# Cross terms of a long convolution added by accumulating transfers, with one pool for product and spectrum buffers and a new order of work

## The chip, the cores and the metric

The kernel runs on one core of a Trainium2 chip. The metric is device time in microseconds (us), the median of several runs. Runs fall into a fast and a slow state (of four, three at a mean granted clock of 0.972 to 0.976, one at 0.84); only fast runs are compared here (the ratios and their intervals; a median given below takes in all runs), and where a trace fell in the slow state, it is said. The granted clock is the share of TensorE's full clock that the profile shows as granted; in the stretches below it lies between 0.50 and 1.00. In this kernel TensorE does the matrix products (PE in the profile, 1780 matmuls in before) into the accumulators called PSUM, the Vector engine (DVE) mostly elementwise work on two inputs (272 of its 406 instructions), the Scalar engine (ACT) activations and evacuations of PSUM (copies out of it), SyncE (SP) and GpSimd (Pool) issue most of the transfers (229 and 16 in before).

## The reference, cut to what matters

A sequence of 2048 positions by 640 channels goes through layer norm, a gated long convolution by Fourier transform, and a SwiGLU feed-forward network (FFN), with residuals:

```python
kv  = shift_conv(k) * v
y   = irfft(rfft(pad(kv)) * rfft(pad(ssm_k)))[:2048] + kv * ssm_D
h   = x + layernorm(x) * y
out = h + (silu(ln(h) @ w_gate) * (ln(h) @ w_up)) @ w_down
```

## The kernel before

The sequence is cut into four blocks (0 to 3), each with its share of convolution and an FFN of 14 feature tiles. Block j's output spectrum is a sum of products of input spectra X and filter spectra (A and B, cut from K) of the blocks up to it. Each transform has two stages on TensorE with a shuffle between them: an on-chip transfer of 160 KB, because the second stage wants other rows together. Names below: `shK21G1` is the shuffle of K, block 2, half 1 of the columns, piece G1 of four; `s2K21G1` the second-stage matmuls that read it; `rs10G2` a shuffle on the way back in block 1; `i1100` the matmuls that read that. These names are the program's; the trace calls all such transfers `sb<-sb`, and they are told apart by their place in their queue, which the program fixes. The shuffled pieces live in rings of three buffers:

```python
P.pool("UK", slots(3, 2 * CW), True)      # shuffled pieces of K, given out in order
P.pool("UX", slots(3, 2 * CW), True)      # shuffled pieces of X
P.pool("E",  slots(5, HW))                # swapped spectra
P.pool("PP", slots(3, HW))                # products
```

Products are multiplied and summed on DVE. `extra` is a cross term that block 2 (the third) computed ahead for block 3 (the fourth), by the eight adds named q4 and q6:

```python
def prods(nm, terms, h, prio, extra=None):
    acc = None
    for n, (a, b_) in enumerate(terms):
        p = (P.tile(f"P{nm}{n}", "PP"), 0)
        ew(p, a, b_, ALU.mult, h, prio, f"m{nm}{n}")
        ...                                # the first is acc, later ones are added on DVE
    if extra is not None:
        ew(acc, acc, extra, ALU.add, h, prio, f"x{nm}")
    return acc
# block 2, after its own sums:
ew(x1, x1, r, ALU.add, h, pr + 5, f"q4{nm}")
ew(a1, a1, q, ALU.add, h, pr + 5, f"q6{nm}")
```

The program isn't written in the order in which it runs. A table in the file gives each of 1219 operations an engine and a planned start time, presumably found by a search outside the chip (the code carries an estimated cost for every operation); the code replays that table: it sorts each engine's instructions by it, hands out pool buffers in that sequence, and adds semaphores. Up to the first FFN, a group of matmuls with a planned wait ahead of it gets filler matmuls. So each engine does its work strictly in the order of the table.

## Time and profile before

| | before |
|---|---|
| median of 4 runs beside the changed kernel | 312.83 us (310.87 to 313.86) |
| span of the profiled run | 308.7 us |
| PE busy, of it filler | 283.5 us, 19.4 us |
| DVE, ACT, Pool busy | 234.8, 187.1, 27.0 us |

The prediction below shows the lines behind this table. For what follows it helps to cut the span at the same points of the program in both kernels: at the first FFN matmul, at the last matmul of `dn0310`, at the first matmul of the third FFN, and at the last matmul of all. `dn0310` ends the down product of one of the first FFN's four row groups; two of the others follow some 10 us later. The stretch up to it is called the first FFN stage below.

### The profile page before, as it was taken

To read this page: it belongs to the slowest core of one execution; us is meant where nothing else is said; L and a number is where in the kernel's file an instruction comes from. 1 tells how busy PE (TensorE), PEld (TensorE's weight loads), DVE (VectorE), ACT (ScalarE), POOL (GpSimd) and SP (SyncE) were. 2 spreads that over 40 slices of the span, in tenths; PEclk is the share of its full clock that TensorE was granted. 3 is DMA by queue.
4 is the path that set the end of the run, shared out by engine and by line. 5 is a ranking of instruction groups with operands and counts; after the bars stand their busy time and mean duration, and the time that the engine had idled before them with its cause. 6 is when DMAs were issued, how large, how long until landed. Compare 5 with 4: busy or idle time off the path is not lost.

```text
span 308.7 us, 4989 instructions
## 1 busy us (share of the span) xinstructions
PE 283.5 (92%) x1780; PEld 167.9 (54%) x1780; DVE 234.8 (76%) x406; ACT 187.1 (61%) x280; POOL 27.0 (9%) x34
## 2 busy tenths in 40 slices
...
GB/s 219 342 193 297 237 220 236 222 142 298 253 274 290 293 268 266 167 252 216 197 236 42 127 227 53 127 151 206 199 111 82 46 46 81 2 0 0 2 85 44
DMA packets 53116, 52.09 MB, mean 169 GB/s; under 512 B 21202, under 2 KB 46163, under 8 KB 53092
## 3 DMA queue, kind: packets, MB, share of 16 engines
...
q10 hardware_dynamic: 1010, 0.79, 0.8%
...
## 4 chain that ended last, share of the span: by engine, by line
PE 62%; DMA 14%; DVE 7%; ACT 7%; SPq 4%; issue 3%; POOL 0%; ACTq 0%; DVEq 0%
PE ps L492 58%; DMA sb<-sb 11%; DVE sb L501 6%; SPq L483 4%; ACT sb L475 3%; PE ps L515 3%; DMA sb<-in_A_ssm_k_dram 2%; DMA sb<-in_A_q_dram 1%; ACT sb L478 1%; ACT sb L778 1%; PE ps L624 1%; ACT sb L790 1%; DVE stt L755 1%; DVE sb L777 0%; POOL stt L768 0%
## 5 line engine op out<-in xcount | busy, mean ns | idle before, releaser
L492 PE MATMUL ps<-sb 128*128 128x320 bf16 (+3 forms) x1128 | 208.9, 336 | 1.1 <-DVE sb L501 1.1
L501 DVE TENSOR_TENSOR sb<-sb 128x1280 bf16<-128x1280 bf16 (+2 forms) x238 | 174.1, 767 | 15.8 <-ACT sb L475 4.7
L492 PEld LDWEIGHTS ps<-sb 128*128 128x128 bf16 (+2 forms) x1128 | 108.6, 98 | 82.3 <-issue 4.7
L475 ACT ACTIVATE sb<-ps 128x640 bf16<-128x640 f32 x131 | 88.7, 712 | 39.1 <-PE ps L492 37.3
L492 PE MATMUL ps<-sb,tab 128*128 128x320 bf16 x450 | 78.2, 303 | 10.3 <-DMA sb<-sb 7.5
L492 PEld LDWEIGHTS ps<-sb,tab 128*128 128x128 f16 x450 | 42.3, 98 | 38.1 <-DMA sb<-sb 7.7
L501 DVE TENSOR_TENSOR sb<-ps,sb 128x640 bf16<-128x640 f32 (+3 forms) x34 | 29.1, 857 | 41.9 <-PE ps L492 40.4
L1034 ACT ACTIVATE sb<-ps 128x1024 bf16<-128x1024 f32 (+2 forms) x32 | 29.3, 916 | 23.7 <-PE ps L492 23.5
L778 ACT ACTIVATE sb<-sb,stt 128x320 bf16<-128x320 bf16 (+1 forms) x34 | 24.0, 728 | 7.1 <-DVE stt L770 4.8
L478 ACT ACTIVATE sb<-ps 128x640 bf16<-128x640 f32 x31 | 21.0, 704 | 10.5 <-PE ps L492 10.4
L515 PE MATMUL ps<-sb 128*128 128x192 bf16 x158 | 19.4, 270 | 7.3 <-ACT sb L475 4.2
L755 DVE BATCH_NORM_STATS2 stt<-sb 128x6 f32<-128x320 bf16 x48 | 22.3, 484 | 0.2
L1050 ACT ACTIVATE sb<-ps 128x1024 bf16<-128x1024 f32 x18 | 18.4, 1025 | 5.6 <-PE ps L492 4.9
L515 PEld LDWEIGHTS ps<-sb 128*128 128x128 bf16 x158 | 14.4, 107 | 12.9 <-ACT sb L475 7.6
L768 POOL TENSOR_TENSOR stt<-stt 128x2 f32<-128x2 f32 (+1 forms) x10 | 11.4, 1138 | 52.6 <-DVE stt L766 42.1
L476 DVE CAST sb<-ps 128x640 bf16<-128x640 f32 (+1 forms) x8 | 6.2, 779 | 7.9 <-PE ps L492 7.9
L804 POOL TENSOR_TENSOR stt<-stt 128x4 f32<-128x4 f32 x2 | 2.6, 1297 | 77.4 <-DVE stt L802 77.4
L790 ACT ACTIVATE sb<-sb 128x640 bf16<-128x640 bf16 x8 | 6.0, 744 | 2.3 <-DMA sb<-in_A_q_dram 2.3
L797 ACT ACTIVATE sb<-sb,stt 128x640 bf16<-128x640 bf16 x8 | 6.6, 832 | 0.0
L777 DVE TENSOR_SCALAR sb<-sb,stt 128x320 bf16<-128x320 bf16 (+1 forms) x14 | 5.5, 395 | 0.9 <-DMA sb<-sb 0.5
L483 POOL DMA_DIRECT2D sb<-in_B_w_down_dram x3 | 2.1, 698 | 32.9 <-DVE sb L501 29.0
L483 POOL DMA_DIRECT2D sb<-in_A_k_dram x2 | 2.1, 1028 | 26.8 <-DVE stt L759 26.8
...
## 6 DMA issues: line engine op xcount, KB each, us to landing
sb<-sb SPq DMA_DIRECT2D x144, 160.0 KB, 2.3
out_dram<-sb SPq DMA_DIRECT2D x16, 160.0 KB, 1.9
...
sb<-in_A_v_dram POOLq DMA_DIRECT2D x4, 320.0 KB, 4.4
...
```

Of the source, the lines that this page charges most:

```text
L475: fns = {"act": lambda a: a.activation(out=dst(), in_=src(), func=ACTF.Copy), "dve": lambda v: v.tensor_copy(out=dst(), in_=src())}
L478: fns = {"act": lambda a: a.activation(out=dst(), in_=src(), func=ACTF.Copy, scale=scale), "dve": lambda v: v.tensor_scalar(out=dst(), in0 ...
L483: fns = [(lambda g, d=d, s=s: g.dma_start(d(), s())) for d, s in subs]
L492: return lambda t: t.matmul(o(), l(), r(), start=st, stop=sp)
L501: return lambda v: v.tensor_tensor(out=o(), in0=a(), in1=b_(), op=op)
L515: P.fill = lambda t, pt: t.matmul(B32(pt, 1, 192), V(GUT, 13 * 512 + 256, 128), V(GUT, 13 * 512, 192), start=True, stop=True)
L755: vec(dve1(CW, False), lambda v: v.bn_stats(st6(l, j, b, c), V(xt, b * D + c * CW, CW)), [(xt, (b, c))], [(ST, ("s", j % 2, b, c))], prio, ...
L768: P.op({"pool": 0.95}, lambda g: g.tensor_tensor(out=y, in0=va, in1=stt[:, 288:288 + hi - lo], op=ALU.pow), c1 + [(ST, "half")], c3, prio, ...
L778: "act": lambda a: a.activation(out=dst(), in_=src(), func=ACTF.Identity, scale=rs(l, j, b), bias=tmv(l, j, 3)[:, b:b + 1])},
L790: P.op({"act": act_c(D) + 0.22}, lambda a, b=b, jt=jt: a.activation(out=V(jt, 0, D), in_=V(xt, b * D, D), func=ACTF.Copy, accum_out=tmv(l, ...
L1034: P.op({"act": act_c(n)}, lambda a: a.activation(out=dst(), in_=src(), func=ACTF.Silu), rd, wr, -1000, name=f"si{j}{i}")
L1050: P.op({"act": act_c(1024)}, lambda a: a.activation(out=V(ut, 0, 1024), in_=B32x2(u, 512), func=ACTF.Copy), [(u, 0), (u, 1)], [(ut, 0)], - ...
```

## The change

Its intent is to relieve DVE: the sixteen adds of cross terms become transfers that add in flight into their destination, issued from Pool. Product and spectrum buffers come from one pool of eight, because a product now lives longer (until the transfer has read it: from issue to landing such a transfer took 3.5 to 7.25 us in the trace of after, where an add on DVE took 0.79 in before). And there is a new order for all of it. The diff, cut:

```diff
+    DACC = "xq"
-        P.pool("E", slots(5, HW))
-        P.pool("PP", slots(3, HW))
+        P.pool("E", slots(8, HW))
+        def acc_dma(dst, a, h, prio, nm):
+            P.op({"pool": 1.0}, [lambda g: g.dma_start(V(dst[0], dst[1], HW), V(a[0], a[1], HW), accum_op=ALU.add)],
+                 cells(a, h) + cells(dst, h), cells(dst, h), prio, dma=(328, 2560), name=nm)
-                p = (P.tile(f"P{nm}{n}", "PP"), 0)
+                p = (P.tile(f"P{nm}{n}", "E"), 0)
-                ew(acc, acc, extra, ALU.add, h, prio, f"x{nm}")
+                if "x" in DACC: acc_dma(acc, extra, h, prio, f"acx{nm}")
+                else: ew(acc, acc, extra, ALU.add, h, prio, f"x{nm}")
-                ew(x1, x1, r, ALU.add, h, pr + 5, f"q4{nm}")
+                (acc_dma(x1, r, ..., f"acq4{nm}") if "q" in DACC else ew(x1, x1, r, ...))
...                                        # q6 likewise; one setup instruction is put first on its engine
 _ORDER = (                                # the whole table is new
```

More of the change, by code (lines that the diff above doesn't have):

```diff
@@ L128, in replay @@
                     self.pools[tl.pool].free.append((max(p.finish for p in tl.touch), tl.base, tl.touch))
+        q = self.order[self.warm.eng]
+        q.remove(self.warm)
+        q.insert(0, self.warm)
+        for i, o in enumerate(q):
+            o.pos = i
         end, cold = 0.6, 6.9
@@ L716, in prods @@
                 else:
-                    ew(acc, acc, p, ALU.add, h, prio, f"a{nm}{n}")
+                    if nm[1] in DACC:
+                        acc_dma(acc, p, h, prio, f"ac{nm}{n}")
+                    else:
+                        ew(acc, acc, p, ALU.add, h, prio, f"a{nm}{n}")
             if extra is not None:
-                ew(acc, acc, extra, ALU.add, h, prio, f"x{nm}")
+                if "x" in DACC:
+                    acc_dma(acc, extra, h, prio, f"acx{nm}")
+                else:
+                    ew(acc, acc, extra, ALU.add, h, prio, f"x{nm}")
             return acc
@@ L915, in conv_half @@
                 x1, a1 = sX(1), sA(1)
-                q = (P.tile(f"q{nm}", "PP"), 0)
+                q = (P.tile(f"q{nm}", "E"), 0)
                 ew(q, x1, Bw, ALU.mult, h, pr + 5, f"q1{nm}")
                 ew(x1, x1, A, ALU.mult, h, pr + 5, f"q2{nm}")
-                r = (P.tile(f"r{nm}", "PP"), 0)
+                r = (P.tile(f"r{nm}", "E"), 0)
                 ew(r, X, a1, ALU.mult, h, pr + 5, f"q3{nm}")
-                ew(x1, x1, r, ALU.add, h, pr + 5, f"q4{nm}")
+                (acc_dma(x1, r, h, pr + 5, f"acq4{nm}") if "q" in DACC else ew(x1, x1, r, ALU.add, h, pr + 5, f"q4{nm}"))
                 ew(a1, Xw, a1, ALU.mult, h, pr + 5, f"q5{nm}")
-                ew(a1, a1, q, ALU.add, h, pr + 5, f"q6{nm}")
+                (acc_dma(a1, q, h, pr + 5, f"acq6{nm}") if "q" in DACC else ew(a1, a1, q, ALU.add, h, pr + 5, f"q6{nm}"))
         def conv_bp(j, c, bp, HTt, pr):
@@ L1127 @@
 _ORDER = (
-    "c-pO030PBC7A7x`kdOtkhwLj^$i4sx*~tb3LLh`B2#6?%vRJFFindy}X>Bc4i+qk&#tpYBE|t1f9c|UNRIS#PDq2NtYf-0)wiPG1b!_X@nXmV}@0|0_yZ4-X"
-    "{`=ntfDi~2h=Dv101AQ+ofrrRg+M_F2!g;<1Ny{!v?eOi0Y3J@fe!=rsX+8CS|?^;*(3A&EKepr$4cnH3*^y$qG1pUjcz^qfDa5b=Fxyafafz&JzxOvH|k+p"
-    "=(8~Rb*~`!4F7SPPj&WG6nNCi<CgwBIq>|+A%Bp30KJE^9(sQbQs9FzKnCD}dKOB+A2#)$jCcUbQ|x%=gkRfwUhMv~B=CQfjN%A9Mils~5Pity=Rowo@a|dU"
-    "co+vj$m1p;{~Lb5?+O5qejC4u1AoXr;0gbtr5>UM{HcBxPD^4UF)JaFm;qS?xdN$z@PP_|2|Ws70+sPCG2cU+z*t~DZ~?%BI`DWb1@<AN4^|IpM7g1#K@Y@)"
@@ L1132 @@
-    "AR@@Su|2UII0|f!<Hvp!TM8D#uE1YMyoTsS-bT_<+tI^;4FC*U58Vr$4xRxqus$FH{SsuvB4Wd_T~HL*2X%vIW0%D?!M=kB;-<#M!>7Xc!kvimu%BUK#A!rx"
-    "{I&SiNG^(xtVeD|DiKo<Y4KI@Juo*s2tNtm5Z{Dyqb{S==t*cMx*ok9U6Y_mIE&em5W=p-9mMWQ>`QFJ+`vx5y+b;OuY!4Fcfhc5)o~}|vf+#2TyQFQBX(C@"
-    "ZfpSNMRX#zB9_EAz(=F^qF=!5z#tR*6S5NLB{sw%;RW%%@%xd3P!VJgQjZj)M<wpZl5v%|d)NZpIoxdAQT%OuKH(cefH;x39P1=ZBJL;FkhYSpl9mxS5V0f*"
-    "X%gu?$wj_RT1mb|9zu?gH<GuJ&yh<g4U{&DFlkKEJxmvA5<W~_OJBeik&tW{OV8RT=w{Cn9TFWBy&-8%dV%^fC4*X?1X8zAI+J!%ebkw>9NIoAg1(k+rb`*k"
@@ L1136 @@
-    "%#T=KbB;4;tWxemRu{KlP$BH)mk7=a>y!PW@k|QiJ8l;DF0+<*m-jJG#qSiJN-h_y7nO)5Y$zunTEl*ubCz>lBolukX_QvUa#df;7RvLLe)S%;RdGP^qjIcj"
-    "s``j{M~XpqL_SNk1cr&P1PQ1%v@BsV;uNYEGlv2}Yccl|P?$+b7`2)X#qJ?rV|UQMrVr)n5!d1GAb9cT;<d;X$bRI@apSOOuu4oH=5S&S_7>WL5#Z+F|AAxR"
-    "C!u@Lqfp0C0rYBg5vm2H#H_{CV>%Ot<6H0(2_1xK37ZmhiPIBz6TeJE5;JgYQVsbS?jZR(B_nA@5}PuT0#Ntk;|Ws2M8dp88TJ#xZNdS9gSeP_g=(hlOxjKf"
-    "Qafk>y^B7UzMD>EjN@+QuHgK_q3~Yk>G%qvfe-Q*@vrcmf-M4Ja!Yb4W(9_vP?sP~+?JStos2z<XOl*fwvgtNgQPanb|Q>qrS40rr*Ecdar<xpQB7Qgi^1E7"
@@ L1140 @@
-    "qlhojjHH`1CH)5)gRZ2N)21;tGgeY5v=F18v5O969$^k;-DY{&vw5TVSNS2{0iIBBn47};fZNNBVHL5KvhJ|P@;>5}@|UqU@#_S?@XrcblVQRm!V$@zCeIbV"
-    "B1Ve)M0Rnv*e}tf?2(j8Orj=9w`5t$MCmo@dKpnlmyVUzN#{z5vhU?@$XXPO<svypK3P6q{+_&2L02{@<|v8EpR}{J2K5)J3A*iSK`KZ4fo6ZICT)rKXqrkd"
-    "*Zfm$PyZ@yo#v+gvSD|IK7(LhX}V~9*DSV1Qa{vvZWwI%HnlN>Yr2@eM9;IVvE&)n*)(>e=@ny#In#XHL^Ch5Fzl~p@*JS+kmrJ9gj4K-dC*xkR-p}-33rq_"
-    "I$g8e*`8j{xojM^pIk;BLD|S+ayDppqz_7+lBP(P=(F{Bqt(=7xNahuTg|!nW_%oB0U>$?DPR(s`U<s~UC0^5+0E%>Q#gwmy^K1(fqRZyB)r6=vh2*!%u?q2"
@@ L1144 @@
-    "%$Y0=dkuf7V3;6IykF2KIL7A-E(kQqPT|<-O}N2J5cMScl8c2`g>Q*);#T2&F<dfEGCk$1l!-E5%7T=ODW9h-lYT3qDoRrLQoZO!(H8L~ak;cz%9Q2FVr2G|"
-    "ZL*UxhD<5{n|!3=o?^42P`O4KqpDD?RmG&vSCKTjv|TEh<_pa#?O^R(-Om=4^;=_{xzXBbZLq^LH(GC5-Nsc$hV8fwY45i0rPb5nj55Y1hL`z1%fvY^*e&8n"
-    "u1HVI+GHeoSh7q~A&)4WYPw>Iyj{*$1QZVG80j$idBs6hf+|jZUwujmSM5|fR0}kE-3oQT_Pkc7ou<2}hO1xFbm>;70%;Ygp|tk2*z|Sj7=4?$R^Jgl!TISP"
-    "!+rgGh7U5_M!$ZG9%EQ-kQ(cZ%QH@7+%jxU?J)8(YBTyXVl5F%lkt?X%v5ZC-+aSrw9T-otxK)ftPWeDv)i)K^_Fdndz{T_Uv9r{w`PvXJeS##>31y5?6ONU"
@@ L1148 @@
-    "8y)Qqg7c!I)-lF`aypzf&d;6QQF+sq;L33tow=@K&b!VEm*2h0HN%Z?AMy?HHRPSin~`7PyPZES2bD9^+njqRr#g@1qj@p8Tm0Gnw{zbt$O<0ySh6zm+ww`-"
-    "R)1Q-)WY6EZBc8{Yk@;SOR+lpldPWLgkVL^{9<H?Txcpd5a=tcEkp-q7P&(ohjSx`BB;88;=`d(SQPo9c6;QrlC08COW9?aC4oU*gGx)w%9b;IiosH@w8T0&"
-    "ZG=~wzc=qfJ~7YjUsQO~uPzV;t^_bedy9T#zssR<=W;E)cHZCBH?<}WKXqN|;<PF0RXS&y#9+<Pm@b*OSza(rG2bvR)E(DxObbj4%~DIM^^RqyGsX6{WtW9)"
-    "t+wuW+;+enX^wq1n{%f--?PGVBI{>Yde-bLcJ^1<f}Hl8#o1T0wK*79o$IDk<?8TU_7FUo9-^l*yC$2K1A4>WCEjg0cf7f|K;9i+W`26!)Vy8!DaF%+C4r=("
@@ L1152 @@
-    "#^UwG?$9^ICyGuK%?X?haDuJDW5Ic0vNl_nm)@OTr*AXOx7WDVn|f>$?ai*ATulzOv)vYNAD#1#N9XIyD{^<aN4Z<wYqHK{DLk)w1ld32Ov#se|K;W8-p>hm"
-    "FXl9PC*-cqZOpr$+nE=W*Xq0FGv^ok=H>hRs|tQBI1%VBP!<x4@ctIR+`rJzEqJlO?c3qI=08yIgFm^jvCv$!uP`gHIB+X~4i*QO1T%wkgWbV<!HVM3#e&e-"
-    "(5etDd^WT;bRmQdRfOc>Vc{L&OX1RRFpQ4872X)05Sbm7oe@I`Cz2GQl#GtFM4|^+(qGb1q8+5IY^~fmOkBkoy1MFm#k7j%DxiAQkk_iK%V(F7E7lCYT;5WF"
-    "9y)%gYxu_DcZX_fEQ61hpRTU2-Zi*n_@E&NhWLkF8tSS1au~O4OX*K#OUqKrCYCjpvuZZgY#nK+ZK}-}v2TQTWamh3ZCc%~y3O^e4YL}OYuDAf>krm58~zP&"
@@ L1156 @@
-    "9!w_"
+    "c-pO02Ut`07Ef+MAdpFRLM9<QAtZq?l8`|LGm~tPEusuJj#jI6(W-T|%2Qjdt94ShrNgT4QLUqj)LE^I;?}yWw!ov-`s`=ldp+mgbIv{YjQ{!F^IZT6215W)"
+    "4}(Eq2o&0_dQE5#^+@0k1bJrt7T6uy&7eMp_Pl`hUN1Pn-95UgPd!)VC7Hl82l%;6FzC5c^gTd&++YX<0`0xJ?;ZyA5x6_`FR5<XqX6g&qK6=Vj=}F!LZL6S"
+    "f!|VJz~m3!?gN1P<^w<9=2gYPf2lb5KZ|!`)_1TT^q|nc1t~}`QV?)A0lfn9-wXnMej}j0-@dy5<mCat?*Rb#f5z^GmcVZ<fmfUfcqyU)`0qy)^8X;(x2KSv"
+    "YQW3<eItRMq53NPfIhqTU-4q0e@FB!{2v><46SGT*JJfU0lZTF8BSb85HuGQ1XX~NfM{S8un7DkxC-0?J_2R{LC}2AKfxWq17H?FhO_|`NC;Q~Gy{)-dteZ<"
@@ new lines @@
+    "D?$x!0|~%;fls4zqBq9aBZ*N>F+W9|ifTuGgWQ8OMGr%tM1jzI&<BB1$W{mvS_a()&55AF1d#C%6%-sX5ZVmwiXg)%P<uo<>>b#;NJ<nrYH!qy$eB@#qnPlw"
+    "VOt_8@FCF;qFZ7f$5;@fV^R@sB5I@WL{E+07X1)5CNc&tkI}^}K`4<;$S$N3wG+uj4Mtr>A4kJ69?XK+{jp};8q5{!VYEG#j$44o5{AN-M!+IRM(&T)Ma_wd"
+    "fKP^g4=suCz^WqMQ4<hrkv9>8k&B|9AT209dI<VGOeJ~)I)G_}<D;RlRv08^C;}9{9`Qa}jD}#}!**hov8C8G*n8Luv9&l6ZXWImj*0KW&&IXkuH$U@o%l(F"
+    "Fku!xjgU_$B#b7UCdh~;;`c-`DL`})w-cuk*AcO#4$@>&8hH|V3hFD&Oj0Eo#+b>RL3$TIgockp#XsWb#rp(yae`zp`6y*OsXt{Ri9lIJUQDr5f1-@0U8Ihp"
@@ new lines @@
+    "9;XeWRnh`+yXoe*mN*(?E}g|#$S`rxyia(lga*EX4-*_0w6e#svN#<~EvKDhjUU0K$Bz@-=ilSLE@~Ek&JZz|#b+{CGjB0ha$ALFkx?c~yr-C!7%N|$q*iQG"
+    "G|M?jWW@r7N|`8uOE1Z2^3jTqVGWTtpkE;j_$9IP;F~FTV`1b{;+I4h?H%G;!ihKx`wLb*bsVRJJ()d+vkV@BKZF}%PR95Vml0!;d*DCCdU5x#AH^<2b1-W#"
+    "_c3R1OK{T(bi5L^5Y>qyqVFS1P^(cVQ8Y{``X~m6{f-bxY$UW1_}JRmCd_usF5*7I7TT9oTO5ztNdAR3mGOX4!lctL&=)hEw4Jmf!gRv6SSqd(_Y{YSvl6@F"
+    "hLOh5BN?;eMzAW`8`yFVjO}ILX4l4_=VWr5xEHu<69_`RU_P&m$KcQ4w+OVtbwZ}-9BMXdEcy;Q54#i#i@ivghd)E!N<mONsYdE*>P=DxIgXx0OJxV?d6Y2}"
@@ new lines @@
+    "Dk+ELCmtkfh;xZUsUk)_Z9d(|8p0YyUquHo8kp}gPcvItBiN7F|6)yyZ{|GZd=o#0caXP~|AgyGsNiF`dhR*yjD#IbGHY7=_V{B75H6iZ;11<2;iLKY`ISP1"
+    "$R~mcy~25-<AM{S7V*#GTuG~>P%4$GB{tDvNxbwm=_cuB*%j$p>2m1>=_x57tCY=_ol3kdi;<5^JS_vs-%4yr#LGv?1@efbsq%};4-|t`$5gGVK=RkgHudt9"
+    "&g3!4ywvIxW;#OIsC<~ZFzunTCjEGNqlT(A>y~P7Yxn35WcpGstE19ar=!!}%iw4g88<Ve`ufZc&076P(*k{qj%8S5fEx-7Q;a*Tmu$<kSLc9ohgyENjItff"
+    "*5y7jY%@yC2h0yGb4<>xgXRv)7uk=nBPd76$y7I|j)O~nBXwZfeDyCW%hK7I;0%R!tj4Wx)F&H0BPEh|l8KZ-l+zSA&B3T<e2{P@VFTw*{P6@n?-C~|elYJW"
@@ new lines @@
+    "e?8A5yuzZg%UNq#0?vHS682U0I4(nQjW=6(ieDzUBA^Nj`Fr_Ggx?Ae2|tKCBI*#1q}oKYM3+PkaW(s>c&Oxpq)kee)u?85qsW&HlFdoP$uRPZvb@A{!6Ly{"
+    "NvC9=jG4Gzc3w6iNh5ulR4HF4pPyt;x}J1dabJE|NmDhb+$kTXG^w+aHz&8LmC9*KXv)BpV9LRiCc_8=J@bpq8-^0&>8!e}9Am5TWF}9KG&xL<O;WRhzKZdL"
+    ";bux%Bz6lsCLt`?FCvS}#cRb6#I+Kr*dyL1;U?dcTvAO^Y*O%LURhn@Ub#E*recV4l}e)8km^*8S2d;VN|CC=YOMOQ8l~Q#RHY`XucoxA(^J1m9iNt#+>sVa"
+    "CuHo%h|m=4FKCLiEd9+4i-w!_siru?rzz6R)V!ae*G$oF(F%1<x(gavdb@6=_Lydd?vhTEIVtn8Hd-IlU)Aq2pp1Uwbi;UKyOC(zZCqgxn>L!LSt^svM9Zqm"
@@ new lines @@
+    "+L8q`zi#%LD@^B2ceBjq6=uGr*-~U7TbPyti`O#7!n7)_Dr>p*to49pw#8>Hw!UeNur0GuY|!jRTdRZO*polfu5k`==v?FT@OgO!+Y7+?L+zdRK>oG7`yQs}"
+    "cz$EyOyA}lTh2abohvyP?H=bAIPbc&UZQWf`-E@4pPf5BcY^P_51B^~5QA@d#=0vC8HG>WBRyxlw}X)ITVZ?=uB6TH2uup1LzxYuLl45UievjZOU4($i=P&c"
+    ">vy!@MfQ5dbg@*@mUTVVnSapEwzC|cyW-vLg#)}Y&u-6m-Y4D?UwJ|?w>_bi=jT@oDup{#Wyzb=M^cBS?@8a4`XH?;?XxtZrbH_+R2kfv6EjH}p$x3POpnqP"
+    "=-xH1(eE-})<+o94JWeT<^|?9^CmOY0=B$n>9iHvwAs#_#WsX(a`v@sy?wF0!g1a%b1ZdCv~IK-Oq8tmtx4H+*^9Hs=03<R%c11l$yt$)&acnklP@VyyC%5a"
```

5 lines of the change are left out of this document (added).

## The prediction

> **What bounds the kernel now.** I read the page's busy shares first, then busy time by stretch of the span, then the list of what TensorE (PE) waited for, then the Vector groups by shape, and last the sizes of the transfers.
>
> ```profile
> PE 283.5 (92%) x1780; PEld 167.9 (54%) x1780; DVE 234.8 (76%) x406; ACT 187.1 (61%) x280; POOL 27.0 (9%) x34
> ...
> L515 PE MATMUL ps<-sb 128*128 128x192 bf16 x158 | 19.4, 270 | 7.3 <-ACT sb L475 4.2
> ```
>
> The page's busy totals and one of its groups. PE is busy 92% of the 308.7 us, but the group of line 515 is filler: dummy matmuls that keep PE running while it has nothing to do, 19.4 us of the 283.5. Useful PE work is 264.1 us, and the other 44.6 us of the span is all that any change of order can win. The stretches show where that lies (columns: stretch, its length, busy us and count of each engine, granted clock, DMA share, GB/s):
>
> ```profile
> 0.00:74.20 74.20, 60.67 (x447) 39.63 (x448) 56.95 (x105) 48.18 (x72) 12.43 (x19) 0.95 0.78 241
> 74.20:145.00 70.80, 67.54 (x432) 40.76 (x431) 65.92 (x114) 52.33 (x74) 7.59 (x8) 1.00 0.86 252
> 145.00:205.00 60.00, 57.25 (x346) 33.08 (x345) 56.51 (x100) 45.77 (x73) 3.99 (x4) 1.00 0.45 148
> 205.00:250.00 45.00, 45.00 (x252) 24.63 (x253) 39.24 (x72) 32.52 (x52) 2.26 (x2) 1.00 0.33 122
> 250.00:303.10 53.10, 53.04 (x310) 29.77 (x307) 15.37 (x22) 8.25 (x9) 0.70 (x1) 1.00 0.11 31
> 303.10:308.70 5.60, 0.00 (x0) 0.00 (x0) 0.80 (x1) 0.00 (x0) 0.00 (x0) 0.69 0.17 60
> ```
>
> At 74.2 us the first matmul of the first block's FFN starts. Before it, PE does 60.7 - 19.4 = 41.3 us of useful work, so 32.9 us are lost to chains of small steps (evacuate, transfer, multiply, add). After it PE lacks only 3.3 + 2.7 + 0 + 0.1 = 6.1 us up to 303.1, and 5.6 us of last add and store end the span. DVE is the close second: 93% busy from 74 to 145, 94% from 145 to 205, 87% to 250. Those 6.1 us have few causes, as the list of PE's waits from 74 us on shows (total, times, longest):
>
> ```profile
> PE ps L492 <- DMA sb<-sb: 4.2, 4, 1.5
> PE ps L492 <- DVE sb L501: 1.4, 2, 1.1
> PE ps L492 <- ACT sb L478: 0.3, 1, 0.3
> ```
>
> So in the blocks that the change touches, only about 1.4 us of PE's idle time is released by a Vector instruction; the largest part is released by on-chip transfers.
>
> [...] The trace of before has no accumulating transfer; [...]its 320 KB loads from DRAM take longer:
>
> ```profile
> sb<-sb SPq DMA_DIRECT2D x144, 160.0 KB, 2.3
> ...
> sb<-in_A_v_dram POOLq DMA_DIRECT2D x4, 320.0 KB, 4.4
> ...
> sb<-in_A_v_dram SPq DMA_DIRECT2D x2, 320.0 KB, 4.1
> ```
>
> [...]Pool's issues in before took 535 to 1028 ns on average beside a DVE that was 90% busy, so I expect no large delay. [...]
>
> **The change, part by part.** (1) The selector is "xq". The ordinary sums of products test the block's digit against it and stay on DVE. Moved are the two "extra" adds of the fourth block (8 instructions: 2 halves of columns, 2 halves of the spectrum, 2 products) and the two cross-term adds of the third (8). All are of this shape:
>
> ```profile
> L501 DVE TENSOR_TENSOR sb<-sb 128x1280 bf16<-128x1280 bf16 x192 | 151.7, 816 | 12.8 <-PE ps L492 4.5 <-ACT sb L475 3.2 <-DMA sb<-sb 3.2
> ```
>
> 151.7 / 192 = 0.79 us each, so DVE loses 16 x 0.79 = 12.6 us (234.8 to about 222). In the built order DVE has only 2 instructions fewer (404 for 406), because 14 to 16 PSUM evacuations and the like move from ACT to DVE: some 14 x 0.5 to 0.8, 7 to 11 us. Net, DVE falls by only 2 to 6 us, and ACT, which had room, by about as much as it hands over. (2) Pool gets 16 issues, about 13 us on an engine that is 9% busy. Data: 16 x 320 KB[...], in a stretch with a DMA share of 0.33 to 0.45. (3) One pool of 8 in place of 5 and 3: no instructions, fewer waits for a free buffer; no PE wait in the list above can be put down to it. (4) The whole order is new, on every engine, and this decides the time. TensorE's useful work is identical.
>
> What the built order shows: before the first FFN matmul the changed kernel has 183 fillers in 19 groups, against 158 in 23. A filler costs about 0.09 us (18 took 1.66 us) and each group has 0.32 us of idle ahead of it (7.3 / 23). So planned waiting there is 25 x 0.09 - 4 x 0.32, about 1 us more. 24 useful matmuls (3.3 us at about 0.136) go behind the FFN's start, and 13 wide Vector instructions of later blocks (10 us) go behind the first block's layer norm, so the FFN starts some 2 us earlier, but that is only moved work. PE's lost time early: +1 us, uncertain by 3.
>
> From 74 us: the 1.4 us wait for the second block's inverse transform should vanish, as PE has 5.4 us of other matmuls there for 3.8. The 1.1 us wait for a Vector add (the third FFN's start) may go, since two of the four residual adds now come earlier. Gain 1.5 to 3 us. Against it, the fourth block: [...]For the first two halves PE has some ten five-matmul FFN groups of about 1.1 us between the last Vector add and the inverse transform, so it is hidden; for the last half only some 4.3 us lie between, then only 20 matmuls (2.7 us) cover evacuation and transfer (0.7 + 2.9 us) before the last transform, where before there were 3.5 us. And 92 matmuls (12.5 us) stand between the last transform and the fourth FFN, where there were 102 (13.9) for a layer norm chain that took about 12.9 us (244.6 to about 257.5). I charge 1 to 2 us. The tail of 5.6 us stays.
>
> Sum: 312.9 + 1 (early) - 2.3 (waits gone) + 1.5 (fourth block) = 313.1 by parts. The new order was, however, found with the freed Vector time in it; since DVE is 93% busy while PE is being filled, I allow 2 to 3 us for small waits in the early stages that fillers hide and I can't name. Prediction 310.5 us.
>
> **Rivals.** (a) The Vector load was the real bound between 74 and 250 us, and 12.6 us less lets everything slide: then 303 to 306 us. For it: 93% busy. Against: PE, which all must pass, lacks only 6.1 us after 74 us, so this can't give over 6 us without a shorter start, and the order shows no shorter start. (b) The transfers land late (6 us or more, from queueing behind swaps or from slow accumulation): each last half stalls PE, which takes its work in a fixed order, 2 to 3 us, and layer norm follows later: 315 to 319 us. For it: no accumulating transfer has been measured here, and Pool issues in order, so one transfer's wait holds the next. Against: only the last quarter is tight. (c) Nothing net, gains and losses cancel: 311 to 314 us. The profile speaks for this most: the removed adds are not on PE's path.
>
> **Range and chances.** Faster by over 2% needs 306.6 us, that is nearly all of the 6.1 us with nothing given back, or a start shorter by several us: 0.14. Slower by over 2% needs (b) or a start that fits badly: 0.07. Range 304 to 316.
>
> **What would show it.** DVE busy near 229 to 232 us and ACT below 187; 16 Pool transfers of 320 KB landing in 3.5 to 5 us; PE useful time unchanged at 264 us; first 256-wide FFN matmul at 70 to 76 us; PE idle from there to the end under 7 us, with its largest wait in the fourth block or at the fourth FFN's start. I am wrong if the first FFN matmul comes later than 78 us or the time lost before it falls by over 3 us, if accumulation takes over 6 us, or if PE waits after 74 us come to more than 9 us.

Cut from it is what no trace of this case shows, with the terms of the author's estimate for one accumulating transfer. That estimate came to 4.3 us with the issue on Pool; only the issue was measured in before (a mean of 779 ns for the four Pool loads of 320 KB). The charge of 1.5 us for the fourth block leaned on it, and the 3.5 to 5 us for landing, under what would show it, is the author's estimate too. The forecast's own sum: 312.9 + 1 - 2.3 + 1.5 = 313.1 us, and 2.6 less for small waits made it 310.5.

## More of the kernel before

The view is busy time by stretch of the kernel before (stretch, length, busy us and count on PE, weight loads, DVE, ACT, Pool, then granted clock, DMA share, GB/s):

```profile
74.20:130.52 56.32, 54.51 (x343) 32.30 (x342) 53.41 (x92) 43.82 (x63) 5.47 (x6) 1.00 0.87 259
130.52:204.96 74.44, 70.27 (x434) 41.50 (x431) 68.98 (x121) 54.28 (x85) 6.11 (x6) 1.00 0.52 163
204.96:302.70 97.74, 97.71 (x559) 54.43 (x560) 54.45 (x91) 40.77 (x61) 2.96 (x3) 1.00 0.21 73
302.70:308.70 6.00, 0.34 (x3) 0.00 (x1) 1.00 (x2) 0.00 (x0) 0.00 (x0) 0.71 0.16 56
```

In the first of these, DVE is busy 53.4 and PE 54.5 of 56.3 us: the first FFN hides the convolutions of blocks 1 and 2, and there is hardly any slack on DVE, nor on PE.

## The result

| | before | after |
|---|---|---|
| median (4 runs each) | 312.83 us | 325.53 us (324.19 to 327.56) |
| ratio of fast runs | | 1.0419 (95% interval 1.0345 to 1.0494) |
| span of the profiled run | 308.7 us | 323.6 us |

The changed kernel is 4% slower; the result is correct. Ratios here and below are one kernel's fast runs against the fast runs of the kernel before on the same chip, so not quite the ratio of the medians. The kernel before had medians of 310.7 to 312.9 us on five chips, so variants are best compared by their ratios.

The page of the kernel after, its busy totals and two groups (filler, and the issue of the accumulating transfers):

```profile
PE 289.4 (89%) x1790; PEld 171.6 (53%) x1805; DVE 232.5 (72%) x404; ACT 179.4 (55%) x266; POOL 43.0 (13%) x53
...
L520 PE MATMUL ps<-sb 128*128 128x192 bf16 x183 | 21.3, 271 | 12.5 <-ACT sb L480 9.1
...
L714 POOL DMA_DIRECT2D sb<-sb x16 | 13.9, 891 | 55.3 <-DVE sb L506 46.8
```

Useful PE time is 289.4 - 21.3 = 268.1 us, where it was 264.1: the matmuls are the same, so some of them ran on a slower clock (a mean of 0.971, where it was 0.983; 15 of the 1805 matmul records are missing from this trace, so 268.1 is rather too low). Idle PE time is 323.6 - 289.4 = 34.2 us, where it was 25.2. The transfers themselves are as expected (the page's list of transfers, KB each and median us from issue to landing):

```profile
sb<-sb SPq DMA_DIRECT2D x145, 160.0 KB, 2.6
sb<-sb POOLq DMA_DIRECT2D x16, 320.0 KB, 4.1
```

The same stretches of the kernel after:

```profile
0.00:73.25 73.25, 59.39 (x447) 40.37 (x448) 52.95 (x100) 37.77 (x58) 8.88 (x15) 0.93 0.74 227
73.25:143.00 69.75, 62.64 (x366) 35.65 (x371) 60.26 (x102) 52.50 (x76) 10.22 (x11) 0.95 0.82 236
...
143.00:215.31 72.31, 69.27 (x425) 41.20 (x427) 66.73 (x115) 52.01 (x81) 14.71 (x17) 1.00 0.76 193
215.31:315.84 100.53, 97.73 (x555) 54.40 (x560) 51.73 (x89) 37.12 (x54) 9.14 (x11) 1.00 0.37 101
...
315.84:323.60 7.76, 0.34 (x3) 0.00 (x1) 0.82 (x1) 0.00 (x0) 0.00 (x0) 0.87 0.06 22
```

| stage | before | after | difference |
|---|---|---|---|
| start to first FFN matmul | 74.20 | 73.25 | -0.95 |
| to the last matmul of `dn0310` | 56.32 | 69.75 | +13.43 |
| to the first matmul of the third FFN | 74.44 | 72.31 | -2.13 |
| to the last matmul | 97.74 | 100.53 | +2.79 |
| to the end | 6.00 | 7.76 | +1.76 |

At the first cut TensorE has done 25 useful matmuls fewer than before (447 with 183 fillers, where it was 447 with 158), at the second it is level within 4. So some 3 of the 13.4 us, as an estimate at the 0.136 us of a matmul that the prediction reads from the trace, are work handed on by the first stage, which itself got only 0.95 us shorter.

The growth at the end isn't TensorE's: the last store lands 1.8 us after its issue in both kernels. The program ends with SyncE waiting for the semaphores of all transfers, and the sixteen new ones need more of them (those waits, before and after: count, ns of one, first and last start in us):

```profile
L259 SPq EVENT_SEMAPHORE  x60: 28/28/28, 304.3 to 308.2; - x60
```

```profile
L264 SPq EVENT_SEMAPHORE  x70: 17/28/28, 317.5 to 323.1; - x70
```

They take 3.9 us in before and 5.6 in after.

Nearly the whole loss lies in the second stage, and the first accumulating transfer is issued at 143.09 us, when that stage is over. So the transfers can't have caused it directly. What TensorE waited for from 74 us on (total, times, longest):

```profile
PE ps L497 <- DMA sb<-sb: 9.7, 6, 2.8
PE ps L497 <- ACT sb L480: 1.4, 5, 0.4
```

These waits for on-chip transfers came to 4.2 us in the kernel before. Four of the six can be seen with the transfer that they wait for in the chain of waits, which is followed back from the last instruction, at each step to what released it (start us, length us, what):

```profile
90.52 4.48 DMA sb<-sb
...
102.75 6.64 DMA sb<-sb
...
121.28 5.56 DMA sb<-sb
...
145.11 6.33 DMA sb<-sb
...
159.41 4.75 DMA sb<-sb
```

The first is `shX11G1` (PE waited 0.82 us at 95 us), then `rs10G2` (2.79 us at 109.6), `shX20G1` (1.71 at 127), the accumulating `acq4200` (a swap of spectra in SP's queue waits for the buffer that it reads, and SP's next twelve issues stand behind that), and `shK21G1` (1.25 at 164). The other two waits are 1.26 us at 153 for the transposing transfers into the second FFN, beside the first two accumulating ones, and 1.87 us at 230 for `shK31G1`. Shuffles with no load beside them landed in some 2.1 us (the four issued from 115.2 to 117.5 us in 2.02 to 2.09); the five shuffles named here took 4.5 to 6.8 us, and beside each of them one or two loads of 320 to 640 KB had been issued (beside `shK31G1` also the accumulating `acxr301`, 0.6 us earlier). `rs10G2` landed almost together with a big one: at 109.39 us, the load `vin21`, issued 0.2 us before it, at 109.15.

PE paid twice for the wait at 109.6 us. Busy time by stretch around it:

```profile
106.80:109.50 2.70, 0.01 (x1) 0.00 (x0) 2.16 (x3) 0.70 (x1) 0.00 (x0) 1.00 1.23 206
109.50:113.00 3.50, 3.41 (x12) 1.54 (x13) 1.67 (x3) 1.00 (x2) 0.00 (x0) 0.56 1.12 348
113.00:116.00 3.00, 3.00 (x18) 1.82 (x18) 2.29 (x4) 2.49 (x4) 0.00 (x0) 0.94 0.33 126
```

After 2.7 idle us, the granted clock is 0.56 for 3.5 us, which cost another 3.5 x 0.44 = 1.5 us. After the wait of 1.71 us at 127 us it is 0.51 from 126.9 to 130 us, but after that of 1.87 at 230 us it is 1.00 from 230 to 233 us.

Which pieces came late is no accident. In the trace of after, in order of issue (us; a ring has three buffers, so the last piece of four takes the buffer of one that must have been read):

| ring | issued, in this order | read by PE at |
|---|---|---|
| X11 | G0 81.1, G2 84.6, G3 89.3, **G1 90.5** | G0 89.9, **G1 95.0**, G2 95.2, G3 105.0 |
| X20 | G0 110.1, G2 118.1, **G1 121.3**, G3 125.3 | G0 119.0, **G1 126.9**, G3 141.4, G2 141.7 |
| K21 | G0 136.4, G2 137.0, G3 158.7, **G1 159.4** | G0 156.9, **G1 164.2**, G3 177.0, G2 179.0 |
| K31 | G2 213.9, G0 221.0, **G1 223.0**, G3 232.5 | G0 225.2, **G1 229.9**, G3 235.9, G2 236.3 |

In all four, G1 is read second and fetched third or last, behind a piece that is needed later, mostly much later. For K21 this is worst: G1 gets the buffer of G0 and can't be issued before PE has read that at 156.9 us, while G2 sits in another buffer from 139.6 to 179.0 us.

### The profile page after: what moved, and what is told of

It reads as the page before. It is cut to its first block, busy times and chain, and to the rows that moved or that the text cites. A ratio compares the mean times of both kernels' runs of the same rounds, so it can differ in the third digit from the quotient of the medians.

```text
span 323.6 us, 5041 instructions
## 1 busy us (share of the span) xinstructions
PE 289.4 (89%) x1790; PEld 171.6 (53%) x1805; DVE 232.5 (72%) x404; ACT 179.4 (55%) x266; POOL 43.0 (13%) x53
## 4 chain that ended last, share of the span: by engine, by line
PE 64%; DMA 12%; DVE 6%; ACT 6%; SPq 5%; issue 3%; POOL 1%; ACTq 0%; DVEq 0%
PE ps L497 57%; DMA sb<-sb 12%; PE ps L520 6%; SPq L488 5%; DVE sb L506 4%; ACT sb L480 3%; ACT sb L483 1%; DVE stt L770 1%; DVE sb L481 1%; ACT sb L1049 0%; ACT L1049 0%; PE ps L629 0%; PE ps L1003 0%; ACTq L488 0%; POOL stt L783 0%
## 5 line engine op out<-in xcount | busy, mean ns | idle before, releaser
L506 DVE TENSOR_TENSOR sb<-sb 128x1280 bf16<-128x1280 bf16 (+2 forms) x222 | 162.1, 764 | 20.3 <-ACT sb L480 9.6
L480 ACT ACTIVATE sb<-ps 128x640 bf16<-128x640 f32 (+1 forms) x125 | 85.0, 712 | 53.8 <-PE ps L497 50.5
L497 PE MATMUL ps<-sb,tab 128*128 128x320 bf16 x450 | 80.0, 306 | 11.4 <-DMA sb<-sb 8.4
L520 PE MATMUL ps<-sb 128*128 128x192 bf16 x183 | 21.3, 271 | 12.5 <-ACT sb L480 9.1
L520 PEld LDWEIGHTS ps<-sb 128*128 128x128 bf16 x183 | 16.9, 108 | 16.9 <-ACT sb L480 12.0
L483 ACT ACTIVATE sb<-ps 128x640 bf16<-128x640 f32 x28 | 19.1, 703 | 10.3 <-PE ps L497 7.4
L793 ACT ACTIVATE sb<-sb,stt 128x320 bf16<-128x320 bf16 (+1 forms) x29 | 20.6, 732 | 5.5 <-DVE stt L785 3.2
L481 DVE CAST sb<-ps 128x640 bf16<-128x640 f32 x14 | 11.5, 823 | 16.5 <-PE ps L497 16.4
L714 POOL DMA_DIRECT2D sb<-sb x16 | 13.9, 891 | 55.3 <-DVE sb L506 46.8
L488 POOL DMA_DIRECT2D sb<-in_B_w_gate_dram x4 | 3.7, 929 | 46.5 <-DVE sb L506 45.7
```

The lines of the kernel that those rows point to most:

```text
L480: fns = {"act": lambda a: a.activation(out=dst(), in_=src(), func=ACTF.Copy), "dve": lambda v: v.tensor_copy(out=dst(), in_=src())}
L481: "dve": lambda v: v.tensor_copy(out=dst(), in_=src())}
L483: fns = {"act": lambda a: a.activation(out=dst(), in_=src(), func=ACTF.Copy, scale=scale), "dve": lambda v: v.tensor_scalar(out=dst(), in0 ...
L488: fns = [(lambda g, d=d, s=s: g.dma_start(d(), s())) for d, s in subs]
L497: return lambda t: t.matmul(o(), l(), r(), start=st, stop=sp)
L506: return lambda v: v.tensor_tensor(out=o(), in0=a(), in1=b_(), op=op)
```

## Experiments

My theory was that the new order costs the time (O), later that it is the order in which the rings are filled (R); the rivals were that the accumulating transfers cost it, that big loads beside small transfers do, or that TensorE is paced elsewhere, so that a wait removed only moves (P).

Eighteen kernels ran. All were correct by the comparison.

### Taking the change apart

**a_dve**: the order and pools of after, the adds back on DVE.

```diff
-    DACC = "xq"
+    DACC = ""                             # and an add that the table gives to Pool goes to DVE
```

> The changed kernel's order on every engine, with the 16 adds back on VectorE at the places where their transfers stood. Theory O (the new order costs the time: some 10.5 of the 13.2 us that TensorE loses more than before are lost between 91 and 143 us, before the first accumulating transfer is issued at 143.1 us): 320 to 326 us, with the waits at about 95, 109.6 and 126.9 us still there. Rival T (the accumulating transfers cost it, by their latency or by crowding the DMA engines): 311 to 315 us.

Measured: 325.61 us, ratio 1.0483 (1.0397 to 1.0569). The same loss without a single accumulating transfer. Its first FFN stage takes 66.44 us at a full clock, against 69.75:

```profile
74.26:140.70 66.44, 59.32 (x366) 34.45 (x371) 59.26 (x102) 52.41 (x76) 10.22 (x11) 1.00 0.85 249
```

From its chain of waits:

```profile
107.88 6.11 DVE sb L508 x9
...
152.69 0.57 SPq L490
...
157.28 6.15 DMA sb<-sb
```

DVE carries most of the chain from 108 to 152 us (it is busy for 32.6 of the 35 us from 110 on), then SP issues one transfer after another, and `shK21G1` is again the one that PE waits for: it lands at 163.43 us, where it was 164.15. The two kernels come to the same point by different roads, one full of adds, the other held by `acq4200`.

**b_acc**: the order and pools of before, the sixteen adds as transfers.

```diff
-                ew(acc, acc, extra, ALU.add, h, prio, f"x{nm}")
+                acc_dma(acc, extra, h, prio, f"acx{nm}")      # q4 and q6 likewise
```

> The order and the two pools of before, with the 16 adds as accumulating transfers. Theory O: 313 to 318 us (only what a late sum costs in the fourth block, since that order left no room for 3.5 us of transfer). Rival T: 321 us or more, as in the changed kernel.

Measured: 343.46 us, ratio 1.1025 (1.0895 to 1.1156). Theory O missed by far. The rival's "321 us or more" covers the number, but not "as in the changed kernel": it is 18 us slower than that. DVE now waits for on-chip transfers; this line in the traces of before, after and b_acc:

```profile
DVE sb L501 <- DMA sb<-sb: 3.2, 3, 2.1
```

```profile
DVE sb L506 <- DMA sb<-sb: 7.3, 7, 2.3
```

```profile
DVE sb L503 <- DMA sb<-sb: 23.1, 9, 4.6
```

Eight of these nine stand before a multiplication that begins within 0.1 us of the landing of an accumulating transfer, and that doesn't use its sum: it needs the product buffer which the transfer reads. A DVE add frees it in 0.8 us, a transfer in 3.5 to 6.9. So the change does need an order made for it.

**b_pool**: the order of before, one pool of eight, the setup instruction first.

```diff
-        P.pool("E", slots(5, HW))
-        P.pool("PP", slots(3, HW))
+        P.pool("E", slots(8, HW))
```

> The order of before, with one pool of 8 buffers in place of 5 and 3, and the zero fill first on VectorE: what is left of the change without the new order and the transfers. Both theories: within 1% of before, 310 to 316 us.

Measured: 310.0 us, ratio 0.9966 (0.9904 to 1.0028). The pool costs nothing and brings nothing.

**b_acc_pool**: b_acc with that pool.

> The order of the kernel before, the 16 adds as accumulating transfers, and the merged pool of eight buffers in place of five and three. Theory H (the 30 us that transfers alone cost in the old order came from the three product buffers, held until a transfer of 5 to 7 us has read them): with eight buffers the Vector engine no longer waits for them, and the time is 325 us or less. Rival: the transfers' latency is itself in the path (the next product and the inverse wait for the sum): 335 us or more.

Measured: 336.41 us, ratio 1.0749 (1.0688 to 1.0811), the rival's number. But its reason is not the rival's: DVE still waits for held buffers,

```profile
DVE sb L507 <- DMA sb<-sb: 26.7, 10, 5.2
```

and again six of these ten end at the landing of an accumulating transfer whose sum the next multiplication doesn't use. In the old order eight shared buffers are as full as five and three. The expectation took the merged pool for a remedy, which it isn't.

### Filling or removing single waits

**a_fill**: after, with fillers in three of the waits, so that the clock stays up.

```diff
+        for o in self.order["pe"]:
+            o.lead = {"s2X11G1": 8, "i1100": 32, "s2X20G1": 20}.get(o.name, o.lead)
...                                        # these fillers read the constant table
```

> The changed kernel with filler matmuls (8, 32 and 20) ahead of the three transforms that wait at 95, 109.6 and 126.9 us. The waits stay. If the low granted clock after the two long ones (0.55 in 109.6 to 113 us, 0.66 in 127 to 132 us) comes from TensorE standing idle, the clock stays at 1.0 there and the kernel gains 2 to 3.5 us: 322 to 323.5 us. If the low clock comes from elsewhere[...], nothing is gained or up to 1 us is lost: 325 to 327 us.

Measured: 329.92 us, ratio 1.0527 (1.0391 to 1.0662), with two of four runs slow. The profiled run was fast (325.83 us). In it the clock is 1.00 from 95 to 145 us, where it fell to 0.56 and 0.51 in after: with the waits filled, the dips are gone. Yet nothing is gained. Two pieces of its chain of waits:

```profile
106.84 2.81 PE ps L524 x32
...
158.86 5.26 DMA sb<-sb
```

The fillers run, and PE reaches the matmuls of `shK21G0` 2.4 us earlier than in after (154.5 us for 156.9). But then it waits 3.6 us instead of 1.25 for `shK21G1`, which stands at the end of a run of SP's issues, goes out only 0.5 us earlier and again lands at 164.12 us. The time that PE won is lost there.

**a_ring**: after, with each late G1 exchanged with a piece that is needed later. Nothing else moves; the ring's buffers follow.

```diff
+        by = {o.name: o for o in self.ops if o.dma}
+        for a, b in [("shX11G1", "shX11G3"), ("shX20G1", "shX20G2"), ("shK21G1", "shK21G2"), ("shK31G1", "shK31G2")]:
+            by[a].start, by[b].start = by[b].start, by[a].start
```

> The kernel after, with four pairs of on-chip shuffles exchanged in the SP queue, so that the spectrum piece that TensorE reads second is also fetched second into its ring of three buffers, and a piece that it reads last is fetched last (shX11G1 with G3, shX20G1 with G2, shK21G1 with G2, shK31G1 with G2). Theory R (the new order fetches these pieces in another order than TensorE reads them, and the waits are the loss): the waits 0.82 at 95 us, 1.71 at 127, 1.25 at 164 and 1.87 at 230 us vanish, and with the one at 127 the slow clock after it (about 1.7 us): 5 to 7 us less, 318.5 to 320.5 us. Rival P (TensorE only arrives earlier at the next wait, as it did in the run with fillers): under 2 us gained, 323.5 to 326 us.

Measured: 319.29 us, ratio 1.0213 (1.0158 to 1.0269). As theory R expected: half of the loss goes, 1.0419 to 1.0213, about 6.4 us.

**a_ring1** and **a_ring3**: only the first exchange, and only the other three.

> The kernel after with only the first of the four exchanges (shX11G1 with G3). If a late shuffle costs more than its own wait because it lets the small transfer behind it fall in with big loads: the wait of 0.82 us at 95 us goes, rs10G2 is issued before kin30 and vin21 and lands in 2.2 us instead of 6.6, so the wait of 2.79 us at 109.6 and its slow clock (1.5 us) go as well: 3 to 5 us less than after, 320.5 to 322.5 us. If each wait stands alone: 0.8 us less or nothing, about 325 us, and the trace still shows i1100 waiting over 2 us.

> The other three exchanges without the first. The wait of 2.79 us at 109.6 stays as it was in after. If the first exchange carried most of the 6.4 us: 323 to 325 us. If the three at 127, 164 and 230 us (1.71 + 1.25 + 1.87 us of waiting and 1.7 us of slow clock) are worth what they show: 319 to 321 us.

Measured: a_ring1 323.16 us, ratio 1.0412 (1.0346 to 1.0478); a_ring3 320.39 us, ratio 1.0225 (1.0158 to 1.0293), two of its four runs slow, its trace among them. The first exchange does in the trace just what was expected of it: `rs10G2` goes out at 101.85, ahead of the load `kin30` at 102.72, and lands in 2.17 us (in after: 102.75, behind `kin30` at 101.26, 6.64 us). PE no longer waits there, and the first FFN stage ends at 137.1 instead of 143.0 us. But in the ratio nothing of these 5.9 us is left that is clear of noise (1.0412 against 1.0419, each uncertain by 0.7 points, some 2 us; the profiled runs differ by 1.8 us). PE's waits:

```profile
PE ps L501 <- DMA sb<-sb: 8.8, 4, 2.5
```

One of 2.5 us is for the transposing transfers into the second FFN, beside the first two accumulating ones; then come `shK21G1` (2.31 us, in after 1.25) and `shK31G1` (2.49, in after 1.87). The three later exchanges carry the gain: with or without them, the first one is worth nothing clear of noise (a_ring3 1.0225, all four 1.0213).

**a_dve_ring**: the exchanges, with all adds on DVE.

> The order of the kernel after with the four exchanges and the 16 adds back on the Vector engine: what the accumulating transfers themselves are worth once the ring waits are away. If the transfers help (what the change was made for), this is 2 us or more slower than the run with exchanges and transfers. If order is everything, the two agree within 1% (3 us). If the transfers hurt (6.3 us of one is in the chain at 145 us of the kernel after), this is faster by 2 us or more.

Measured: 321.78 us, ratio 1.0320 (1.0271 to 1.0369), against 1.0213 on the same chip with transfers. With the rings in order, the transfers help by about 1%, as the first of its three expectations said: what the change was made for shows once the late pieces are out of the way.

**a_ring_x**: the exchanges, only the eight cross terms of the fourth block as transfers (`DACC = "x"`).

> The exchanges, with the eight q adds (from 143 us) back on the Vector engine and the eight cross terms left as transfers. If the q transfers delay the FFN's transposing transfers at 150 us (TensorE waited 2.5 us for these beside acq6200 and acq4200 in the run with small loads), 1 to 2 us less than with all sixteen, 317 to 318.5 us. If the Vector engine needs the relief in the third block, 1 to 2.5 us more, 320 to 322 us (all sixteen back on Vector: 321.78 us).

Measured: 318.78 us, ratio 1.0223 (1.0171 to 1.0275). No difference to all sixteen, and between the two ranges expected. Its trace shows what the exchanges leave: PE's waits for on-chip transfers are down from 9.7 us to

```profile
PE ps L503 <- ACT sb L486: 3.0, 8, 0.9
PE ps L503 <- DVE sb L512: 2.0, 3, 1.0
PE ps L503 <- DMA sb<-sb: 2.0, 2, 1.2
```

In return the waits for ACT and DVE have grown: over all their lines they come to 8.1 us from 73 us on, where after has 2.3. So rival P has a part in it: most of the waiting only moved. What stays won in this trace goes with the clock, which is 1.00 in its first FFN stage (73.16 to 138.43 us), where after had 0.95.

**a_ring_small**: the exchanges; `kin30` and `vin21` shortened, two weight loads moved to a quiet moment. Its output is wrong, which doesn't matter for the time.

```diff
-  V2(kt, 0, CW, 7, CW) ... [D, 7]
+  V2(kt, 0, CW, k, CW) ... [D, k]        # k = 1 for kin30; vin21 likewise 1 of 4
+  by["wd3"], by["wd9"]: start after the second kvm30, and wait for it (some 113 us)
```

> As the run before, and the loads that land beside the small shuffles taken away: kin30 loads one row group of seven and vin21 one of four (a wrong result on purpose), wd3 and wd9 are issued at about 113 us instead of 120.7, when the transfer engines are idle. Theory C (loads from the Pool queue beside a shuffle make it 5 to 6.6 us instead of 2.1 and TensorE waits for it): rs10G2 lands by about 106 us, the wait of 2.79 us at 109.6 and the 1.5 us of slow clock after it go too: 4 us less than the run before, about 314 to 317 us. Rival P: the same as the run before within 1.5 us.

Measured: 318.82 us, ratio 1.0233 (1.0180 to 1.0286): the rival's number, no gain over a_ring. `rs10G2` landed in 2.32 us, but by a_ring1 the exchange alone brings that. The moved weight loads now slowed `shK20G0` (PE waits 1.6 us at 119 us). The comparison passed this result although some inputs were stale, so for these inputs it can't tell a wrong term of that size, and correctness of the sums isn't proved by it.

**a_ring_fill**: the exchanges, and the 32 fillers at `i1100`.

> The kernel after with the four exchanges, and 32 filler matmuls of 192 columns at the wait of 2.8 us for rs10G2 (109.6 us). If the slow clock after that wait still costs something now that the ring waits are gone, about 1.5 us less than the run with the exchanges alone (319.29 us), so 317 to 318.5 us. If TensorE only arrives earlier at the next wait, as in the run with fillers and the old fetch order: the same within 1 us. The trace also gives the one of this variant in the fast state that is missing so far: I expect no wait of TensorE above 0.5 us at 95, 127, 164 and 230 us, and one of about 1 to 2.5 us for the transposing transfers hx12 and hx13 near 150 us, beside the first two accumulating ones.

Measured: 322.43 us, ratio 1.0345 (1.0289 to 1.0400), 1.3 points worse than a_ring; neither expectation held. The wait for which the fillers were meant no longer exists (`rs10G2` lands at 105.14 us in this trace), so their 2.8 us are pure cost, and `shK20G1` then goes out behind two weight loads, takes 5.33 us and makes PE wait 3.0 us. Fillers belong to one timing.

**b_ring**: the kernel before with two exchanges of its own.

```diff
+        for a, b in [("shX20G1", "shX20G2"), ("shK21G1", "shK21G3")]: ...
```

> The kernel before with two of its own pairs exchanged: shX20G1 with G2, shK21G1 with G3. Theory R: the waits of 0.75 us at 114.4 and 1.46 us at 140.2 vanish, 1.5 to 2.5 us less, 309 to 310 us against 311.5 (ratio 0.992 to 0.995). Rival P: nothing, ratio 0.998 to 1.002.

Measured: 310.75 us, ratio 0.9983 (0.9936 to 1.0029). Both waits are gone from the trace, and others appear: PE's waits for DVE come to 3.6 us, where they were 2.4, 0.96 us of it before the second FFN. The rival was right here. A likely reason, not tested further: in the kernel before, DVE sets the pace in this stage (53.4 of 56.3 us busy), so PE's waits there cost nothing.

### Which stretch of the new order carries the loss

**h140** and **h106** are hybrids. All that the kernel before starts up to a cut keeps its engine, order and sequence of buffers; the rest follows the order of after, with the transfers. The cuts lie at 140 and 106 us of the planned times in before's table. The expectations speak of 142 and 107 us of its trace, but TensorE reaches these points in the trace at about 154 and 120 us.

```python
head  = start_before < cut
order = where(head, before, after shifted to begin at the cut)     # engine and start of each operation
```

> A hybrid: every operation that the kernel before starts up to its third block's FFN entry (about 142 us of its trace) in the order, on the engine and in the buffers' sequence of before; everything later in the order of the kernel after, with all sixteen accumulating transfers and the merged pool. At this cut only 10 of 1219 operations lie on different sides in the two orders. Theory O (the loss is the new order of the part before the first accumulating transfer): 311 to 316 us, ratio 0.995 to 1.012. Rival T (the later part, its order or its transfers, carries a good part of the 13 us): 319 us or more.

> The same hybrid with an earlier cut: the order of before up to about 107 us of its trace, that of after from there (8 operations on different sides). It splits the early loss in two. In the trace of after, 5 to 6 us of the lost time of TensorE lie before this cut and 6 to 7 between the two cuts. If each stretch carries its own loss, this lies between: 316 to 320 us. If the loss needs the earlier part (the late start of the block sets the late loads), 312 to 315 us. If the middle stretch carries it all: 321 us or more.

Measured: h140 316.98 us, ratio 1.0142 (1.0067 to 1.0218), one of four runs slow; h106 323.49 us, ratio 1.0396 (1.0335 to 1.0458). The first FFN stage of both traces:

```profile
74.90:131.28 56.38, 54.47 (x341) 32.42 (x343) 53.19 (x91) 43.83 (x63) 6.49 (x8) 1.00 0.85 254
```

```profile
76.16:138.46 62.30, 57.02 (x345) 33.26 (x347) 52.57 (x92) 45.41 (x65) 5.35 (x7) 0.97 0.82 246
```

h140 lies just above theory O's range; h106 lies where the middle stretch carries it all. Of 4.2 points, 0.2 belong to the part before about 120 us, 2.5 to that from there to about 154 us, and 1.4 to what comes later, each uncertain by about a point. In h106 the pieces of X11 and X20 and the loads of the down weights are still in the order of before, and the loss is there all the same. Of the four rings it is K21 whose pieces lie in the middle part. That fits a_ring1 and a_ring3, but K21 was not exchanged alone.

**h140_dve**: h140 with `DACC = ""`.

> The hybrid cut at about 142 us with the sixteen adds on the Vector engine: what the transfers are worth by themselves, in an order that was made for them and behind an unspoilt first part. From the traces so far, TensorE lost 6.7 us from 148 us on with adds on Vector and the exchanges, and 1.7 to 2.8 us with transfers: 3 to 5 us more than the hybrid with transfers, 315 to 320 us. If transfers are worth nothing: within 1 us of it.

Measured: 315.45 us, ratio 1.0134 (1.0083 to 1.0186), the same as with transfers, against my 3 to 5 us more. The comparison isn't quite fair to the transfers: in h140 the buffers fall differently, and DVE waits for on-chip transfers come to

```profile
DVE sb L508 <- DMA sb<-sb: 18.4, 8, 4.2
```

as in b_acc, where after has 7.3 us. Four of these eight waits, 11.0 us, end at the landing of an accumulating transfer whose buffer is needed. So the 1.4 points of the later part need not all be the order's own; some may be made by the seam, which no run separates.

### Candidates to beat both

**h140_best**: h140, two exchanges, 30 fillers.

> A candidate to beat all: the hybrid cut at about 142 us, with two exchanges of shuffles (shX20G1 with G2 in the part of before, shK31G1 with G2 in the part of after, whose wait was 1.87 us), and 30 fillers in the wait of 3.4 us at 62.8 us. I expect 1 to 3 us less than the hybrid: 309 to 313 us, ratio 0.985 to 1.003. If waits only move on: the same as the hybrid.

Measured: 317.58 us, ratio 1.0165 (1.0090 to 1.0240), two of six runs slow. Nothing gained on h140, although the waits for `shX20G1` and `shK31G1` are gone from the trace.

**b_best**: the kernel before with the merged pool, the two exchanges, one load held back and 30 fillers where the clock dipped.

```diff
+        o.lead = {"s2K10G1": 33}.get(o.name, o.lead)
+        by["vin31"]: start after gm15, and wait for it (some 186 us)
```

> A candidate to beat both: the kernel before with the merged pool of eight, the two exchanges, 30 more filler matmuls in the wait of 3.4 us at 62.8 us (the clock fell to 0.53 after it), and vin31 held from 180.6 to about 186 us, so that rs21G2 and rs21G3 go alone (wait of 1.38 us at 188 us). The four terms are about 2.2 + 1.5 + 1.4 = 5 us if each is real and none comes back; I expect 2 to 4 us less than before, ratio 0.987 to 0.994. If waits only move on, ratio 0.996 to 1.002.

Measured: 309.42 us, ratio 0.9918 (0.9862 to 0.9973) over 5 rounds. It beats both, the kernel before by 0.8%, within what I expected (0.987 to 0.994), though less than the four terms add up to. One term didn't come: PE still waits 1.52 us for `shK21G1`, 1.46 in before, although it was exchanged. The fillers do what they should (before, then b_best):

```profile
60.00:63.00 3.00, 0.23 (x2) 0.20 (x3) 1.45 (x3) 0.48 (x1) 0.00 (x0) 0.99 0.89 315
63.00:66.00 3.00, 2.86 (x13) 1.14 (x12) 1.86 (x5) 2.13 (x4) 0.00 (x0) 0.50 0.05 20
```

```profile
60.00:63.00 3.00, 3.00 (x37) 2.91 (x35) 1.56 (x3) 0.87 (x3) 0.00 (x0) 1.00 1.00 349
63.00:66.00 3.00, 2.32 (x15) 0.88 (x13) 2.19 (x6) 2.54 (x4) 0.18 (x1) 1.00 0.27 106
```

The clock stays at 1.00 where it fell to 0.50, and the wait of 1.4 us at 188 us is gone as well. Which of the parts carries the gain was not separated.

## Why the prediction was wrong

The number was 310.5 us with a range to 316, the result 325.53: wrong in the direction, and outside the range.

- **"PE's lost time early: +1 us, uncertain by 3"** held. The first FFN matmul came at 73.25 us, and the time before it without useful PE work is 73.25 - (59.4 - 21.3) = 35.2 us, where it was 32.9. h106 puts only 0.2 points of the loss into the order before about 120 us.
- **"From 74 us: ... Gain 1.5 to 3 us"** is the step that failed. It listed the waits of before that would vanish and asked of none of the new order's transfers whether it comes in time for its reader. The two waits named did go from the trace (the first is one of block 2, the third). But PE's waits for on-chip transfers rose from 4.2 to 9.7 us: in their place stand four shuffles fetched later than PE's reading order wants, and what they delay. Exchanging these alone took 2.1 of 4.2 points off, the three later ones 1.9. The built order, which I had before predicting, shows the sequence in each ring and PE's sequence. I counted matmuls between adds and transforms in it, but didn't compare those two lists.
- **"I allow 2 to 3 us for small waits in the early stages"** was a gain, granted because the order "was found with the freed Vector time in it". That is how 313.1 by parts became 310.5. An order found by a model need not be better on the chip; its first FFN stage was 13.4 us longer, some 3 us of it work handed on. The clock dip after a wait was not in the working at all: a_dve and after run 366 matmuls each in that stage in 59.3 us at a clock of 1.00 and in 62.6 us at 0.95, so dips cost 3.3 us there. As a_fill shows, this is not simply added to the time.
- **"I charge 1 to 2 us" for the fourth block** was undersized: that stage grew by 2.8 us, with a wait of 1.87 us for `shK31G1`. Whether the adding has a share in this wait isn't settled: the accumulating `acxr301` ran beside that piece, which took 6.82 us; in a_dve, without it, the piece took 5.49 us and PE waited only 0.44, but PE also came later and the landing was the same (229.9 us). "The tail of 5.6 us stays" was undersized too: by the cut used here it grew from 6.0 to 7.8 us. It is 6.4 us in both a_dve and a_dve_ring, so 1.4 us go with the transfers: their semaphores, which SyncE waits for at the end (a_dve has 62 of those waits, after 70).
- **The cost of a transfer** was right as a number: 4.3 us by the estimate, a median of 4.1 measured (3.5 to 7.25). So was Pool's issue, 0.89 us (0.84 to 1.20), with no large delay beside DVE. That DVE would fall only to 229 to 232 us was nearly right (232.5). That the adds give nothing net, as rival (c) says, held in this order: a_dve against after, and h140_dve against h140, differ by less than a point, within noise; with the rings in order the transfers are worth 1.1 points.
- **Rival (b)**, late transfers, named the right kind of wait for the wrong transfers: those that came late were mostly the shuffles, which both kernels have, not the new accumulating ones.
- Of the falsifiers, "PE waits after 74 us come to more than 9 us" is the one that fired: those for on-chip transfers alone are 9.7 us. The largest was expected in the fourth block or at the fourth FFN; it came at 109.6 us. (Three of the sixteen accumulations also took over 6 us.)

What stays open is the second half, about 2 points with the rings in order. One part is plain in the counts: the new order does less in the first stage (ACT 37.8 us for 48.2, DVE 53.0 for 57.0) and hands that on, but the first stage hardly got shorter. In the first FFN stage DVE then has 60.3 us of work where it had 53.4, so that stage can't be as short as 56.3 us in this order. a_dve_ring fits:

```profile
72.71:137.55 64.84, 59.68 (x366) 34.39 (x371) 59.10 (x102) 52.51 (x76) 11.60 (x11) 1.00 0.86 254
```

59.1 us of DVE in 64.8. But no run moved only that work back, so this is argued, not shown. h106, with DVE work as in before and still 62.3 us, shows that it isn't the only cause.
